# Seven block products in layer 2 for two of four experts, layer 1 in longer periods, activation sums on GpSimd

## The chip, the cores and the metric

The kernel runs on one core of one Trainium2 chip. The metric is the device time of one execution in microseconds (us); a kernel's figure is the median of its runs. Before the change it was 541.23 us (three runs, 541.15 to 541.62). All numbers below come from those timings, or from one profiled execution per kernel. Chips differ a little, so the kernel before ran beside every experiment on the same chip.

The engines are called TensorE (PE in the profile, its weight loads PEld), VectorE (DVE), ScalarE (ACT), GpSimd (POOL) and SyncE (SP, which here only issues DMA).

## The reference

Linear attention for 8 batches of 8 heads, followed by a mixture of four experts over 4608 tokens of 512 features.

```python
def phi(x):                               # feature map
    return np.where(x > 0, x, np.exp(x) - 1.0) + 1.0
# q, k, v: (8, 8, 576, 64)
kv  = einsum('bhsd,bhse->bhde', phi(k), v);  z = sum(phi(k), axis=2)
num = einsum('bhsd,bhde->bhse', phi(q), kv); den = einsum('bhsd,bhd->bhs', phi(q), z) + 1e-6
x   = (num / den) transposed to (4608, 512)
p   = domain_probs / (domain_probs.sum(-1) + 1e-9)
out = sum over e of p[:, e] * (max(x @ w1[e], 0) @ w2[e])   # w1: 4 x 512 x 1024, w2: 4 x 1024 x 512
```

The kernel cuts the tokens into nine tiles of 512. Tiles 0 to 7 are the first 512 rows of each batch. Tile 8 is made of the 64 rows that each batch has left ("leftover" rows). A *unit* is one tile and one expert, written (tile, expert); the experts are 0 to 3. Attention of batch j+1 is done in small steps between the products of tile j. Tile 0 and unit (1,0) are plain start-up work.

## The kernel before: the parts that matter

Layer 1 of a unit is done, from unit (1,1) on, with seven block products instead of eight (Winograd's form of Strassen's scheme): x and w1 are cut into 2 x 2 blocks, some sums of blocks are made beforehand (`token_sums` for x on GpSimd, `weight_sums` for w1 once), and the results are combined when they leave the accumulator (PSUM). A block row of 128 hidden features is called a chunk here. Layer 2 is plain: four token quarters, eight products each.

```python
def token_sums(j):                       # 4 instructions on GpSimd per tile
    ...
    nc.gpsimd.tensor_tensor(out=t[:, 0], in0=b12, in1=b11, op=AO.subtract)
    ...
class Block:                             # one chunk: 7 products of 2 x (128x256)
    def a(self):
        product(self.b, a_block(e, 0, 0, k), x[:, 0:2, 0:NH], True)
        u1 = self.copy("u1")             # ScalarE, 128x256
        product(self.e5, ...); product(pa2, ...)
        add_relu(self.h1[:, 0:NH], pa2, u1)   # VectorE, 128x256
    # b6, c, d: the other four products
def layer2_half(j, e, ns, hT, half):     # plain layer 2, 4 of 8 products of 128x512
    for fj in range(half * FC // 2, (half + 1) * FC // 2):
        nc.tensor.matmul(out=py, lhsT=hT[fj][:, ns * P : (ns + 1) * P], rhs=w2_sb[e][:, fj, :], ...)
    ...
    nc.vector.scalar_tensor_tensor(out=acc, in0=py, scalar=pscal, in1=acc, op0=AO.mult, op1=AO.add)
# feature map: exp on ScalarE, max(x,0)+1 on GpSimd, the minimum of both on VectorE
eng.tensor_scalar(dst, src, 0.0, 1.0, AO.max, AO.add)          # eng = GpSimd
nc.vector.tensor_tensor(out=dst, in0=ee[:, 0:n], in1=dst, op=AO.min)
```

Of the kernel before, what the change touches and what calls it, by code (L numbers as in the profile page):

```python
# [20 lines left out]
def kernel(  # L21
# [16 lines left out]
    P = 128  # L38
# [13 lines left out]
    NHT = 18  # L52
    NACC = 5
    NH = NT // 2
    FH = FC // 2
    BIG = 3.0e38
# [6 lines left out]
    warm_in = pconst.tile([P, NT], FP16, tag="warm", name="warm_in")  # L63
    nc.vector.memset(warm_in, 0.0)


    NB2 = 2
    kvzs, kls, qls = [], [], []
    for i in range(NB2):
        kl = pconst.tile([P, NPAIR, P], FP16, tag=f"kl{i}", name=f"kl{i}")  # L70
        nc.vector.memset(kl, 0.0)
        kls.append(kl)
        kvz = pconst.tile([P, NPAIR, 2, DE], FP16, tag=f"kvz{i}", name=f"kvz{i}")
        nc.vector.memset(kvz, 0.0)
        kvzs.append(kvz)
        qTl = pconst.tile([P, 2, 2, P], FP16, tag=f"ql{i}", name=f"ql{i}")
        nc.gpsimd.memset(qTl, 0.0)
        qls.append(qTl)
# [10 lines left out]

    px = ctx.enter_context(tc.tile_pool(name="px", bufs=1))  # L90
    xT_left = px.tile([P, DC, NT], FP16, tag="xTl")

    praw = ctx.enter_context(tc.tile_pool(name="praw", bufs=6))
# [61 lines left out]
    class Batch:  # L155
# [19 lines left out]
        def load(self, name, g, eng=nc.sync, parts=1):  # L175
            src = {"q": q, "k": k, "v": v}[name]
            t = praw.tile([P, HG, CM, D], FP32, tag="raw", name="rawb")
# [9 lines left out]
        def alloc(self):  # L187
# [3 lines left out]
            self.vl = pa.tile([P, HG, DE], FP16, tag="vl", bufs=2, name="vl")  # L191
# [4 lines left out]
            self.x = pa.tile([P, NPAIR, CM, P], FP16, tag="xsb", bufs=1, name="x_sb")  # L196
# [3 lines left out]
        def phi(self, name, g, part=0, parts=1, eng=nc.vector):  # L200

            n = HG // parts
            h0 = g * HG + part * n
            src = self.raw[name, g][:, part * n : (part + 1) * n]
            dst = (self.qp if name == "q" else self.kp)[:, :, h0 : h0 + n, :]
            dst = dst.rearrange("p c h d -> p h c d")
            ee = pa.tile([P, HG, CM, D], FP16, tag="phie", bufs=2, name="ee")
            nc.scalar.activation(ee[:, 0:n], src, AF.Exp)  # L208
            eng.tensor_scalar(dst, src, 0.0, 1.0, AO.max, AO.add)  # L209
            nc.vector.tensor_tensor(out=dst, in0=ee[:, 0:n], in1=dst, op=AO.min)  # L210
# [9 lines left out]
        def left_kv(self):  # L220
            el = pa.tile([P, HG * D], FP16, tag="el", bufs=2, name="el")
            kt = pa.tile([P, HG * D], FP16, tag="ktl", bufs=1, name="ktl")
            rk = self.rl[:, 0].rearrange("p h d -> p (h d)")
            nc.scalar.activation(el, rk, AF.Exp)
            nc.gpsimd.tensor_scalar(kt, rk, 0.0, 1.0, AO.max, AO.add)
            for u in range(2):
                us = slice(u * HP, (u + 1) * HP)
                nc.vector.tensor_tensor(
                    out=self.kl[us, 2 * u : 2 * u + 2].rearrange("p a d -> p (a d)"),
                    in0=el[us],  # L230
                    in1=kt[us],
                    op=AO.min,
                )
            nc.gpsimd.tensor_copy(self.vl[:, :, 0:D], self.rl[:, 1])

        def left_q(self, eng=nc.vector):
            el = pa.tile([P, HG * D], FP16, tag="el", bufs=2, name="elq")
# [3 lines left out]
            eng.tensor_scalar(qd, rq, 0.0, 1.0, AO.max, AO.add)  # L241
# [61 lines left out]
        def nd(self, i0, n):  # L303

            ps = aps([P, 3, 2, DE], FP32, "psum_nd")
# [56 lines left out]
    def layer1_group(j, e, fj, hT, ph=None, dcs=range(DC)):  # L362
# [10 lines left out]
        if dcs[-1] == DC - 1:  # L373
            ht = pm.tile([P, NT], FP16, tag="ht", bufs=NHT, name="ht")
            nc.scalar.activation(ht, ph, AF.Relu)  # L375
            hT.append(ht)
        return ph

    pys = {}

    def layer2_half(j, e, ns, hT, half):
        if half == 0:
            pys[ns] = ppm.tile([P, Dm], FP32, tag="py", bufs=2, name="py")
        py = pys[ns]
        for fj in range(half * FC // 2, (half + 1) * FC // 2):
            nc.tensor.matmul(  # L386
                out=py,
                lhsT=hT[fj][:, ns * P : (ns + 1) * P],
# [4 lines left out]
        if half == 0:  # L393
            return
        if e == 0:
            accs[j, ns] = pm.tile([P, Dm], FP32, tag="acc", bufs=NACC, name="acc")
        acc = accs[j, ns]
        pscal = p_sb[:, j, ns, e : e + 1]
        if e == 0:
            nc.scalar.activation(acc, py, AF.Identity, scale=pscal)  # L400
        else:
            nc.vector.scalar_tensor_tensor(  # L402
                out=acc,
                in0=py,
                scalar=pscal,
                in1=acc,
                op0=AO.mult,
                op1=AO.add,
            )
        if e == E - 1:  # L410
            if j < B:
                nc.sync.dma_start(
                    out=out_b[j, 0:SM].rearrange("(p c) d -> c p d", c=CM)[ns],
                    in_=acc,
                )
            else:
                for u in range(2):
                    nc.sync.dma_start(
                        out=out_b[2 * ns + u, SM:S],
                        in_=acc[u * HP : (u + 1) * HP],  # L420
                    )
# [10 lines left out]
    def weight_sums(e, part):  # L432
# [8 lines left out]
        else:  # L441
            nc.vector.tensor_tensor(
                out=w[:, 0:2, f2], in0=w[:, 0:2, f1], in1=w[:, 0:2, f2], op=AO.subtract
            )

# [27 lines left out]
    class Block:  # L473


        def __init__(self, j, e, k, hT):
            self.j, self.e, self.k, self.hT = j, e, k, hT

        def copy(self, tag):
            u = pm.tile([P, NH], FP32, tag=tag, bufs=2, name=tag)  # L480
# [3 lines left out]
        def a(self):  # L484
            j, e, k = self.j, self.e, self.k
            x, t = xT_of(j), tts[j]
            self.b = ppm.tile([P, NT], FP32, tag="b", bufs=2, name="pb")[:, 0:NH]
            self.e5 = ppm.tile([P, NT], FP32, tag="e", bufs=2, name="pe")[:, 0:NH]
            pa2 = ppm.tile([P, NT], FP32, tag="s", bufs=2, name="pa2")[:, 0:NH]
            self.h1 = pm.tile([P, NT], FP16, tag="ht", bufs=NHT, name="ht1")  # L490
            self.h2 = pm.tile([P, NT], FP16, tag="ht", bufs=NHT, name="ht2")
            self.hT[k], self.hT[FH + k] = self.h1, self.h2
            product(self.b, a_block(e, 0, 0, k), x[:, 0:2, 0:NH], True)
            u1 = self.copy("u1")
            product(self.e5, s_block(e, 0, k), t[:, 0], True)
            product(pa2, a_block(e, 0, 1, k), x[:, 2:4, 0:NH], True)
            add_relu(self.h1[:, 0:NH], pa2, u1)

        def b6(self):
            product(self.b, s_block(self.e, 1, self.k), tts[self.j][:, 1], False)  # L500
            self.u2 = self.copy("u2")

        def c(self):
            product(self.b, a_block(self.e, 1, 0, self.k), tts[self.j][:, 2], False)
            u3 = self.copy("u3")
            add_relu(self.h2[:, NH:NT], self.e5, u3)

        def d(self):
            e, k = self.e, self.k
            product(self.b, a_block(e, 1, 1, k), tts[self.j][:, 3], False)  # L510
            nc.scalar.activation(self.h2[:, 0:NH], self.b, AF.Relu)
            product(self.e5, s_block(e, 2, k), xT_of(self.j)[:, 2:4, NH:NT], False)
            add_relu(self.h1[:, NH:NT], self.e5, self.u2)
# [5 lines left out]
    def layer2(j, e, hT):  # L519
        return [(layer2_half, j, e, ns, hT, h) for ns in range(NSUB) for h in range(2)]  # L520

    def unit(j, e, hT=None, phs=()):

        hT = [] if hT is None else hT
        return layer1(j, e, hT, phs) + layer2(j, e, hT)

    def run(pieces, steps=(), lead=0):

        n, m = len(pieces) - lead, len(steps)
        done = 0  # L530
        for i, g in enumerate(pieces):
            g[0](*g[1:])
            while done < m and (i + 1 - lead) * m >= (done + 1) * n:
                steps[done][0](*steps[done][1:])
                done += 1

    ORDER = [("q", 0), ("k", 0), ("v", 0), ("q", 1), ("k", 1), ("v", 1)]

    def batch_steps(bt, nxt):


        def load(n, g):
            if nxt is not None:
# [6 lines left out]
        def nd(i0, n):  # L550
# [6 lines left out]
            [(bt.phi, n, g, part, 2, nc.gpsimd)] + ([(load, n, g)] if part else [])  # L557
# [6 lines left out]
        for i in range(4):  # L564
            st[2 + i].append((bt.vcast, i // 2, i % 2, 2))
            if i % 2:
                st[2 + i].append((load, "v", i // 2))
        st.append([(bt.left_kv,)])
        st.append([(bt.left_q, nc.gpsimd), (load_left,), (bt.dma_qTl,), (bt.kv, 0)])
        for i0 in range(0, NPAIR * CM, 3):  # L570
            st.append([(nd, i0, min(3, NPAIR * CM - i0))])
        st[10].append((bt.kv, 2))
# [3 lines left out]
    def warm(n):  # L576

        warm_ps = ppm.tile([P, NT], FP32, tag="py", bufs=2, name="warm_ps")
        for i in range(n):
            nc.tensor.matmul(  # L580
                out=warm_ps, lhsT=warm_in[:, 0:P], rhs=warm_in, start=True, stop=True
# [4 lines left out]
    with tc.manual_schedule(  # L586
# [19 lines left out]
        b0.phi("q", 1, eng=nc.gpsimd)  # L606
# [24 lines left out]
        hT = []  # L631
# [34 lines left out]
        for i, g in enumerate(pieces):  # L666
# [3 lines left out]
            if r in (1, 3, 5) and e == 3:  # L670
                weight_sums(e, r // 2)
            elif r in (9, 11, 13) and e < 3:
                weight_sums(e, r // 2 - 4)
            elif r == 15 and e in (1, 2):
                weight_sums(e, 3)
            while done < len(steps) and T0 + TG * (i + 1) >= steps[done][0]:
# [5 lines left out]
        hT = []  # L682
# [10 lines left out]
        for n, g in ORDER:  # L693
# [4 lines left out]
        for g in layer1(1, 0, hT, phs):  # L698
            g[0](*g[1:])
        weight_sums(0, 3)  # L700
        weight_sums(3, 3)
        turn["aps"], turn["ph"] = ["s"], None


        l2 = layer2(1, 0, hT)
        units = [(j, e) for j in range(1, NTILES) for e in range(E) if (j, e) > (1, 0)]
        blocks = []
# [84 lines left out]
```

## Time and profile before

| before | value | read from |
|---|---|---|
| median | 541.23 us | timings |
| span profiled | 539.9 us, granted clock 0.98 | page |
| TensorE busy | 95% | page, part 1 |
| one unit without attention work (tiles 7, 8) | 13.02 us | timeline: spacing of the first products of units |
| one tile with attention work (2, 4, 5, 6; tile 3 took 56.29) | 55.88 us | the same |

First the busy times on the page (part 1: us busy, share of the span, instructions), and the chain of waits by engine (part 4).

```profile
PE 512.7 (95%) x3449; PEld 324.3 (60%) x3449; DVE 316.0 (59%) x718; ACT 286.1 (53%) x722; POOL 173.8 (32%) x158
...
PE 76%; DMA 11%; ACT 3%; DVE 3%; issue 3%; POOL 2%; SPq 1%; DVEq 0%; ACTq 0%; POOLq 0%
```

TensorE is the bound: it is busy nearly all the time, and 76% of the chain that ended last is its work. A matmul's end is modelled in the profile, so rates are read from starts. Here is TensorE's timeline in tile 7 (start us, us, engine, line, operation; x2 means two products merged).

```profile
440.23 0.38 PE L386 MATMUL py<-w_0_84,ht_5630 128*128 128x512 f16 x1
440.45 0.38 PE L386 MATMUL py<-w_0_84,ht_5669 128*128 128x512 f16 x1
...
441.10 0.38 PE L461 MATMUL pb<-xT,w_1_81 128*128 128x256 f16 x2
441.31 0.38 PE L461 MATMUL pe<-tt,s_1_90 128*128 128x256 f16 x2
```

A product of 512 columns takes 0.217 us and one of 256 columns 0.108 us (two in 0.217), with no gaps. Layer 2 of a unit is therefore 32 x 0.217 = 6.93 us. Three groups of the two engines that the change loads (last figures: us busy, mean ns of one, then idle time before them):

```profile
L402 DVE SCALAR_TENSOR_TENSOR acc<-py,p_sb,acc 128x512 f32<-128x512 f32 x108 | 81.0, 750 | 54.5 <-PE py L386 54.3
L453 POOL TENSOR_TENSOR tt<-xT 128x512 f16<-128x512 f16 x7 | 8.1, 1156 | 172.2 <-DMA xT<-x_sb 156.3
...
L209 POOL TENSOR_SCALAR kp<-rawb 128x512 f16<-128x512 f32 x24 | 45.5, 1922 | 0.0
```

VectorE adds a quarter of layer 2 in 0.750 us; GpSimd makes one token sum in 1.156 us, and a share of a feature map in 1.922 us.

### The profile page before, as it was taken

To read this page: it belongs to the slowest core of one execution; us is meant where nothing else is said; L and a number is where in the kernel's file an instruction comes from. 1 tells how busy PE (TensorE), PEld (TensorE's weight loads), DVE (VectorE), ACT (ScalarE), POOL (GpSimd) and SP (SyncE) were. 2 spreads that over 40 slices of the span, in tenths; PEclk is the share of its full clock that TensorE was granted. 3 is DMA by queue.
4 is the path that set the end of the run, shared out by engine and by line. 5 is a ranking of instruction groups with operands and counts; after the bars stand their busy time and mean duration, and the time that the engine had idled before them with its cause. 6 is when DMAs were issued, how large, how long until landed. Compare 5 with 4: busy or idle time off the path is not lost.

```text
span 539.9 us, 9645 instructions
## 1 busy us (share of the span) xinstructions
PE 512.7 (95%) x3449; PEld 324.3 (60%) x3449; DVE 316.0 (59%) x718; ACT 286.1 (53%) x722; POOL 173.8 (32%) x158
## 2 busy tenths in 40 slices
PE   6599998989999999999999999999999999999996
PEld 2344454556666666666666666666666666666662
DVE  4422486457664767476756675667656655655463
ACT  5354375683576357544764476446754455445540
POOL 4722512930960195008600780059003300000000
PEclk9599999999999999999999999999999999999999
DMA  9999935675165206710472039200511010011003
GB/s 262 135 208 209 237 125 182 168 224 126 38 185 168 41 6 162 221 33 16 126 244 46 16 93 264 59 17 31 87 26 26 20 59 2 1 38 42 2 0 79
DMA packets 80736, 54.31 MB, mean 101 GB/s; under 512 B 46032, under 2 KB 73680, under 8 KB 80688
## 3 DMA queue, kind: packets, MB, share of 16 engines
q1 hardware_dynamic: 71648, 41.77, 29.1%
q0 software_dynamic: 9040, 11.93, 11.7%
q8 instruction: 27, 0.44, 0.4%
q14 instruction: 21, 0.17, 0.1%
HBM read 45.16 MB, written 9.44 MB: 101 GB/s over the span
## 4 chain that ended last, share of the span: by engine, by line
PE 76%; DMA 11%; ACT 3%; DVE 3%; issue 3%; POOL 2%; SPq 1%; DVEq 0%; ACTq 0%; POOLq 0%
PE py L386 39%; PE pb L461 18%; PE pe L461 10%; DMA w_3_87<-in_moe_w_dram 4%; DMA w_1_85<-in_moe_w_dram 3%; DMA rawb<-in_q_dram 2%; ACT ee L208 1%; PE psum_nd L308 1%; PE ph L366 1%; DMA ql_75<-qlp 1%; DMA rl<-in_k_dram 1%; SPq L168 1%; PE psum_kv L273 1%; POOL qp L209 1%; DVE x_sb L296 1%
## 5 line engine op out<-in xcount | busy, mean ns | idle before, releaser
L402 DVE SCALAR_TENSOR_TENSOR acc<-py,p_sb,acc 128x512 f32<-128x512 f32 x108 | 81.0, 750 | 54.5 <-PE py L386 54.3
L453 POOL TENSOR_TENSOR tt<-xT 128x512 f16<-128x512 f16 x7 | 8.1, 1156 | 172.2 <-DMA xT<-x_sb 156.3
L209 POOL TENSOR_SCALAR qp<-rawb 128x512 f16<-128x512 f32 (+1 forms) x25 | 49.4, 1998 | 1.0 <-DMA rawb<-in_q_dram 1.0
L209 POOL TENSOR_SCALAR kp<-rawb 128x512 f16<-128x512 f32 x24 | 45.5, 1922 | 0.0
L208 ACT ACTIVATE ee<-rawb 128x512 f16<-128x512 f32 (+1 forms) x56 | 37.9, 692 | 3.6 <-DMA rawb<-in_q_dram 2.6
L400 ACT ACTIVATE acc<-py,p_sb 128x512 f32<-128x512 f32 x36 | 24.7, 687 | 23.7 <-PE py L386 23.7
L375 ACT ACTIVATE ht<-ph 128x512 f16<-128x512 f32 x40 | 23.2, 598 | 21.7 <-PE ph L366 21.5
L461 PEld LDWEIGHTS <-w_1_81 128*128 128x128 f16 x256 | 25.0, 98 | 9.8
L461 PEld LDWEIGHTS <-w_3_83 128*128 128x128 f16 x256 | 24.6, 98 | 8.0
L461 PEld LDWEIGHTS <-w_2_82 128*128 128x128 f16 x256 | 24.4, 98 | 8.2 <-issue 2.5
L461 PEld LDWEIGHTS <-w_0_80 128*128 128x128 f16 x224 | 21.9, 98 | 8.5
L296 DVE TENSOR_TENSOR x_sb<-psum_nd,recip 128x384 f16<-128x384 f32 (+2 forms) x52 | 25.2, 485 | 1.8
L461 PEld LDWEIGHTS <-s_1_90 128*128 128x128 f16 x192 | 18.7, 98 | 11.0 <-issue 2.3
L386 PEld LDWEIGHTS <-ht 128*128 128x128 f16 x160 | 15.3, 98 | 15.6
L461 PE MATMUL pb<-tt,w_2_82 128*128 128x256 f16 x128 | 24.4, 273 | 0.0
L461 PE MATMUL pb<-tt,w_3_83 128*128 128x256 f16 x128 | 24.4, 273 | 0.0
L461 PE MATMUL pb<-tt,w_1_81 128*128 128x256 f16 x128 | 24.4, 272 | 0.0
L461 PEld LDWEIGHTS <-s_3_92 128*128 128x128 f16 x192 | 18.7, 98 | 8.5
L461 PEld LDWEIGHTS <-s_0_89 128*128 128x128 f16 x168 | 16.4, 98 | 9.5 <-issue 1.3
L210 DVE TENSOR_TENSOR qp<-ee,qp 128x512 f16<-128x512 f16 (+1 forms) x28 | 14.8, 545 | 12.2 <-ACT ee L208 5.4
L461 PEld LDWEIGHTS <-s_2_91 128*128 128x128 f16 x192 | 18.1, 98 | 6.1 <-issue 0.5
L461 PE MATMUL pb<-tt,w_0_80 128*128 128x256 f16 x112 | 21.4, 273 | 0.0
(1621 smaller groups left out, 1406.1 us busy)
## 6 DMA issues: line engine op xcount, KB each, us to landing
out_dram<-acc SPq DMA_DIRECT2D x32, 256.0 KB, 2.5
rawb<-in_q_dram SPq DMA_DIRECT2D x14, 512.0 KB, 4.2
rawb<-in_k_dram SPq DMA_DIRECT2D x14, 512.0 KB, 6.3
rawb<-in_v_dram SPq DMA_DIRECT2D x13, 512.0 KB, 5.7
w_0_80<-in_moe_w_dram POOLq DMA_DIRECT2D x4, 256.0 KB, 7.0
w_0_84<-in_moe_w_dram POOLq DMA_DIRECT2D x2, 512.0 KB, 11.0
w_1_81<-in_moe_w_dram POOLq DMA_DIRECT2D x2, 512.0 KB, 15.0
w_1_85<-in_moe_w_dram POOLq DMA_DIRECT2D x2, 512.0 KB, 18.8
```

Of the source, the lines that this page charges most:

```text
L168: eng.dma_start(out=self.rl[u * HP : (u + 1) * HP, i], in_=src[b, u * HG : (u + 1) * HG, SM:S].rearrange("h r d -> r h d"),)
L208: nc.scalar.activation(ee[:, 0:n], src, AF.Exp)
L209: eng.tensor_scalar(dst, src, 0.0, 1.0, AO.max, AO.add)
L210: nc.vector.tensor_tensor(out=dst, in0=ee[:, 0:n], in1=dst, op=AO.min)
L273: nc.tensor.matmul(out=ps[:, i], lhsT=self.kp[:, c, hs], rhs=self.vp[:, c, hs], start=(c == 0), stop=False,)
L296: nc.vector.tensor_tensor(out=dst.rearrange("p n (u d) -> p n u d", u=2), in0=ps[:, 0:n, :, 0:D], in1=recip[:, 0:n].broadcast_to([P, n, 2, ...
L375: nc.scalar.activation(ht, ph, AF.Relu)
L386: nc.tensor.matmul(out=py, lhsT=hT[fj][:, ns * P : (ns + 1) * P], rhs=w2_sb[e][:, fj, :], start=(fj == 0), stop=(fj == FC - 1),)
L400: nc.scalar.activation(acc, py, AF.Identity, scale=pscal)
L402: nc.vector.scalar_tensor_tensor(out=acc, in0=py, scalar=pscal, in1=acc, op0=AO.mult, op1=AO.add,)
L453: nc.gpsimd.tensor_tensor(out=t[:, 0], in0=b12, in1=b11, op=AO.subtract)
L461: nc.tensor.matmul(out=ps, lhsT=lhsT(kc), rhs=rhs[:, kc], start=first and kc == 0, stop=kc == 1, skip_group_check=True,)
```

## The change

The intent is to take TensorE time out of layer 2, as layer 1 already does. For experts 1 and 3 (`SE`) layer 2 is also done by seven block products: 56 products of 256 columns instead of 32 of 512. To do so GpSimd makes four sums of activations per half unit (`hidden_sums`), and VectorE adds each of 14 half-bank results into the output. Layer 1 goes from one to two chunks per PSUM bank (fewer, larger copies and sums). The feature maps leave GpSimd for VectorE and ScalarE. Layer 2 follows layer 1 half a unit behind instead of a quarter.

```diff
+    SE = (1, 3)
...
+    def hidden_sums(h):
+        hs = pm.tile([P, 3, 2, NH], FP16, tag="hs", bufs=2, name="hs")
+        a11, a21 = h[:, :, 0, 0:NH], h[:, :, 0, NH:NT]
+        a12, a22 = h[:, :, 1, 0:NH], h[:, :, 1, NH:NT]
+        nc.gpsimd.tensor_tensor(out=hs[:, 0], in0=a21, in1=a22, op=AO.add)
+        nc.gpsimd.tensor_tensor(out=hs[:, 1], in0=hs[:, 0], in1=a11, op=AO.subtract)
+        nc.gpsimd.tensor_tensor(out=a21, in0=a11, in1=a21, op=AO.subtract)
+        nc.gpsimd.tensor_tensor(out=hs[:, 2], in0=a12, in1=hs[:, 1], op=AO.subtract)
+    def layer2_product(j, e, hT, hss, p, i):      # product p of token half-quarter i
+        if p == 2:
+            pys[i] = new_py()                     # one bank for all seven products of i
+        run, side = pys[i][:, 0:DH], pys[i][:, DH:Dm]
+        ...                                       # 4 products of 128x256, then one add
+        add_acc(j, e, ns, ps, ds, False)          # VectorE, 128x256
...
         def phi(self, name, g, part=0, parts=1):
...
-            eng.tensor_scalar(dst, src, 0.0, 1.0, AO.max, AO.add)
-            nc.vector.tensor_tensor(out=dst, in0=ee[:, 0:n], in1=dst, op=AO.min)
+            if self.b < 3:
+                nc.vector.tensor_scalar(dsth, src, 1.0, 1.0, AO.add, AO.max)
+                nc.vector.tensor_tensor(out=dsth, in0=eeh, in1=dsth, op=AO.min)
+            else:
+                nc.scalar.activation(dsth, src, AF.Identity, bias=1.0)
+                nc.vector.scalar_tensor_tensor(
+                    out=dst, in0=dst, scalar=1.0, in1=ee, op0=AO.max, op1=AO.min)
...
+        NSLOT, LAG = 7, 6                         # a unit is 14 slots
+                for d in range(2):
+                    work[at + (d - 1) * NSLOT].append((sums, d))
+                l2 = [(layer2_product, j, e, hT, hss, p, i) for p in (2, 5, 1, 6, 7, 3, 4) for i in range(2)]
...
-        b0.phi("q", 1, eng=nc.gpsimd)
+        b0.phi("q", 1)
```

Also changed: input buffers 6 to 4, output accumulators (`acc`) 5 to 4, one buffer instead of two for leftover k, q and v and for k'v, x in buffers shared with other tiles, leftover k and q to VectorE, k'v of a batch in one step.

## The prediction

> **What bounds it now.** TensorE: on the page busy 95% of the 539.9 us span at a granted clock of 0.98, and 76% of the chain of waits. In the timeline of tiles 7 and 8 (no attention work) a 128x256 product takes 0.108 us, a 128x512 one 0.217 us, without gaps: 13.03 us per (tile, expert) unit. A batch period with attention work is 55.9 us (spacing of equal pieces in the chain); 4 x 13.0 plus about 2.2 us of attention products leave 1.6 us lost per batch. The waits show part of it (ScalarE copy of k'v 0.6 us, VectorE 0.3 us).
>
> **What it removes.** Layer 2 of one unit is 32 products of 512 columns, 6.93 us. Seven block products are 56 of 256 columns, 6.07 us. That saves 0.87 us in 16 units: 13.9 us, all on TensorE and so on the critical path. Weight loads (98 ns) still hide behind 108 ns products, as layer 1 shows.
>
> **What it adds and moves.**
> - VectorE: 14 scaled adds of 128x256 instead of 4 of 128x512 (0.750 us each; estimate for half the elements 0.48 us): 6.8 instead of 3.0 us per such unit. Layer 1's sums, 6 of 512 instead of 12 of 256, save about 0.9 us per unit. Feature-map work comes over from GpSimd. VectorE goes from 36 to about 42 us per batch of 53, and to about 95% in units with seven products and attention work. The Trainium skill, "VectorE: DVE Perf Modes", perf-mode tier table, puts fp32 PSUM operands at 1x; 0.750 us for 512 columns agrees.
> - ScalarE: about even, 32 us per batch.
> - GpSimd: loses 16 maxima of 1.92 us per batch, gains 8 hidden sums per such unit; token sums of that size take 1.155 us, so 9.2 us per unit of 12.6. The Trainium skill, "GPSIMD Engine Reference", section 3.1, gives about 2.6 cycles per element for two inputs; the trace agrees.
>
> **New waits.** The products of a token half accumulate in one bank, so VectorE must have read a half bank before TensorE returns two slots (1.7 us) later; after product and add about 0.55 us of queueing is allowed. At 95% some of it is missed: 0.65 us on 12 units, 8 us in all. The first hidden sum has about 2.6 us, its chain needs about 2.3. At the very end nothing covers it: +0.6 us.
>
> **Regained.** Layer 1 in longer periods gives copies more slack, and k'v comes a step ahead of its use: about 5 us. At the start GpSimd's 3.63 us pass, which delayed the weight loads and x, goes to VectorE (0.69 us): about 2 us, less if DMA, saturated there, gives nothing back, or if four input buffers instead of six delay batch 1.
>
> **Sum.** 541.2 - 13.9 - 5 - 2 + 8 = about 528 us; range 519 to 538. Chances: faster by over 2% 0.60, within 2% 0.36, slower 0.04.
>
> **What would show it.** Right: in tiles 7 and 8 two units cost 12.15 and two 13.0 us; batch period 52.5 to 54; TensorE's waits in the batches name VectorE's adds into acc; GpSimd 23 us per batch; first layer 1 product 2 us sooner. Wrong: product spacing over 0.108 us in layer 2; batch period near 55.
>
> **What would make it wrong.** VectorE over 100% in units 1 and 3, or slowed by GpSimd's reads (in this trace a VectorE sum beside GpSimd work took 1.10 instead of 0.68 us): then 540. Hidden sums late behind the token sums: a stall per tile. Or fewer waits than I think: then 519.

## The result, and the profile after

The changed kernel takes 541.48 us (median of four runs, 539.74 to 542.04); the kernel before took 541.42 us beside it. The ratio is 0.9996, with a 95% interval of 0.9972 to 1.002: the same. Here and below a ratio is the mean time of one kernel's fast runs over that of the other's of the same rounds, so it is not quite the ratio of the medians quoted.

The page of the changed kernel, the same two lines as before:

```profile
PE 503.6 (93%) x3833; PEld 363.0 (67%) x3833; DVE 366.7 (68%) x729; ACT 279.8 (52%) x514; POOL 215.0 (40%) x221
...
PE 76%; DVE 11%; issue 4%; DMA 3%; ACT 3%; POOL 1%; SPq 0%; DVEq 0%; ACTq 0%; POOLq 0%
```

The span is 539.5 us. TensorE has less to do, and VectorE's share of the chain has gone from 3% to 11%. The equal 76% of TensorE misleads: until 97 us, before unit (1,1), the chain of the kernel before runs 51 us through DMA (weight loads mostly) and that of the changed kernel 12 us, with TensorE's products in their place. From 97 us on TensorE's part fell from 402 to 351 us and VectorE's rose from 8 to 49 us (the chain of `--critical`, summed). That says where to look; what was lost is read below from the lengths of units. The groups that answer to those above:

```profile
L423 DVE SCALAR_TENSOR_TENSOR acc<-py,p_sb,acc 128x256 f32<-128x256 f32 (+1 forms) x268 | 137.7, 522 | 28.5 <-PE py L512 18.4
L486 POOL TENSOR_TENSOR hs<-h 128x512 f16<-128x512 f16 x32 | 37.0, 1158 | 198.2 <-DVE h L560 198.2
```

The costs of the instructions were as foreseen: 1.158 us per hidden sum, and 0.475 us per 128x256 add (the mean of the group within tile 3). So the question is where the time went. The table gives the start of layer 1 of a unit, taken from TensorE's timeline (its first product `pb<-xT`), as differences between the kernels.

| stretch | before | after | difference |
|---|---|---|---|
| start to (1,1) | 96.91 | 94.91 | -2.00 |
| (1,1) to (2,0) | 44.87 | 49.77 | +4.90 |
| (2,0) to (7,0), five tiles | 279.78 | 273.78 | -6.00 |
| (7,0) to (8,3), seven units | 91.15 | 88.36 | -2.79 |
| (8,3) to the end of the span | 27.16 | 32.64 | +5.48 |

(About 1.1 us of the last row is no loss. It is an estimate from the product times: layer 2 follows a quarter unit later than before, so more of it is left when the last layer 1 begins, and so are three products of a block of layer 1 that is now twice as large. Each column is one trace; the first row is within the scatter of such traces, see the experiments.) In tiles 7 and 8 a unit takes 12.62 instead of 13.02 us, that is 0.80 us less for each pair of units: the saving of the products is there. It is lost in three other places.

**Place 1: unit (1,2) takes 22.81 instead of 18.02 us.** TensorE's and then GpSimd's timeline there:

```profile
116.78 0.39 PE L282 MATMUL psum_kv<-vp,kp 128*128 128x130 f16 x4
123.19 0.27 PE L289 MATMUL psum_kv<-vl,kl_63 128*128 128x130 f16 x1 [6.02 <-POOL vl L243]
```

```profile
118.03 1.15 POOL L486 TENSOR_TENSOR hs<-h 128x512 f16<-128x512 f16 x1 [1.49 <-DVE h L560]
119.26 1.15 POOL L487 TENSOR_TENSOR hs<-hs,h 128x512 f16<-128x512 f16 x1
120.37 1.20 POOL L488 TENSOR_TENSOR h<-h 128x512 f16<-128x512 f16 x1
121.53 1.20 POOL L489 TENSOR_TENSOR hs<-h,hs 128x512 f16<-128x512 f16 x1
122.68 0.46 POOL L243 CAST vl<-rl 128x256 f16<-128x256 f32 x1
```

TensorE stands still for 6.02 us before the product of batch 2's leftover rows. It needs `vl`, a cast of 0.46 us on GpSimd that stands in GpSimd's queue behind the hidden sums of unit (1,1), which themselves wait for late results of layer 1. The Trainium skill, "PSUM — Partial Sum Buffer", section "Engine vs sequencer instructions", calls the queues of ScalarE, VectorE and GpSimd strictly first in, first out, and this trace agrees: the cast's input had been loaded long before (issued at 91.35 us), and it started 0.05 us before the last sum ended and not sooner.

The pause is not all that unit (1,2) lost. TensorE's granted clock fell while it stood still (`--windows`):

```profile
core 0: us, PE busy (x) PEld busy (x) DVE busy (x) ACT busy (x) POOL busy (x), PEclk, DMA share, GB/s
120.80:127.40 6.60, 4.21 (x30) 3.58 (x30) 3.91 (x8) 1.95 (x6) 2.34 (x3) 0.50 0.35 90
```

At this clock of 0.50 four products of 256 columns were 0.85 us apart (124.88 and 125.73) instead of 0.435. From the spacing of its starts the unit's 22.81 us are about 10.7 of products at full clock, 9.7 of waits (6.2 at this pause, 3.5 at layer 1's sums and copies before it) and 2.3 of slower products: an estimate.

**Place 2: unit (j,0) of each tile 2 to 6 takes 14.23 us.** Its products need about 12.6 us (an estimate from 0.435 us per four of 256 columns and 0.217 us per one of 512). Waits of TensorE from 85 to 535 us (total us, times, longest), the changed kernel:

```profile
PE py L512 <- DVE acc L423: 6.1, 12, 0.8
PE psum_kv L289 <- POOL vl L243: 6.0, 1, 6.0
```

TensorE returns to a bank before VectorE has read it. From start to start unit (3,0) lost 1.64 us against its products' times, and unit (3,1), which takes 13.01 us, another 0.42. VectorE's timeline at the longest such wait, in unit (3,0), and below it GpSimd's:

```profile
210.88 0.47 DVE L423 SCALAR_TENSOR_TENSOR acc<-py,p_sb,acc 128x256 f32<-128x256 f32 x1
211.28 1.50 DVE L222 SCALAR_TENSOR_TENSOR qp<-qp,ee 128x512 f16<-128x512 f16 x1
212.70 0.86 DVE L423 SCALAR_TENSOR_TENSOR acc<-py,p_sb,acc 128x256 f32<-128x256 f32 x2
```

```profile
208.31 1.68 POOL L487 TENSOR_TENSOR hs<-hs,h 128x512 f16<-128x512 f16 x1
209.96 1.16 POOL L488 TENSOR_TENSOR h<-h 128x512 f16<-128x512 f16 x1
211.07 1.16 POOL L489 TENSOR_TENSOR hs<-h,hs 128x512 f16<-128x512 f16 x1
212.17 0.87 POOL L243 CAST vl<-rl 128x256 f16<-128x256 f32 x1
```

The feature map's instruction on VectorE (L222, two operands in SBUF) usually takes 0.69 us. Here it took 1.50: it began 0.21 us after a hidden sum had begun, and the sum ended at 212.23, so 0.95 of the 1.50 us fell beside it. Then GpSimd's cast, begun at 212.17, took 0.87 instead of 0.46 us. This fits the Trainium skill, "SBUF — State Buffer", section "Who interferes with whom": a VectorE instruction with two SBUF inputs and a GpSimd instruction that reads SBUF exclude each other for the whole of the one that came first. The adds from PSUM, with only one tensor input in SBUF, are not touched (0.475 us on average in tile 3, and the same 0.475 us in run 8 below, where GpSimd's sums are short), as that section also says.

**Place 3: the end.** The chain of waits over the last products of unit (8,3):

```profile
525.38 0.61 PE py L512 x4
...
526.01 0.49 DVE acc L423
...
526.55 0.61 PE py L512 x4
...
527.18 0.49 DVE acc L423
...
527.72 0.61 PE py L512 x4
```

TensorE and VectorE take turns. Each of the two banks is filled in 0.61 us (four products and their way out), then read in 0.49 us, then filled again: 1.17 us per turn, in which TensorE has only 2 x 0.43 = 0.87 us of work. With no layer 1 beside it nothing fills the gap; over seven turns about 2.1 us are lost. At the end all four results become ready together, and SyncE's queue issues eight stores one behind the other (first fence: before, second fence: after; from the timeline of SP, where the second figure is the length of the whole group).

```profile
530.81 6.29 SPq L418 DMA_DIRECT2D out_dram<-acc  x8
```

```profile
531.65 5.04 SPq L410 DMA_DIRECT2D out_dram<-acc  x8
```

Before, VectorE's last add ended at 535.97 and the span 3.9 us later; after, it ended at 533.53 and the span 5.9 us later, with the stores still being issued.

### The profile page after: what moved, and what is told of

Same layout as the page of the kernel before. It is cut to its first block, busy times and chain, and to the rows that moved or that the text cites. A ratio compares the mean times of both kernels' runs of the same rounds, so it can differ in the third digit from the quotient of the medians.

```text
span 539.5 us, 10086 instructions
## 1 busy us (share of the span) xinstructions
PE 503.6 (93%) x3833; PEld 363.0 (67%) x3833; DVE 366.7 (68%) x729; ACT 279.8 (52%) x514; POOL 215.0 (40%) x221
## 4 chain that ended last, share of the span: by engine, by line
PE 76%; DVE 11%; issue 4%; DMA 3%; ACT 3%; POOL 1%; SPq 0%; DVEq 0%; ACTq 0%; POOLq 0%
PE py L432 24%; PE pb L576 16%; PE py L512 14%; PE pe L576 8%; PE ph L377 6%; PE ps L576 4%; DVE acc L423 4%; DVE h L560 2%; DVE qp L222 1%; PE psum_kv L282 1%; DMA xT<-x_sb 1%; DVE x_sb L305 1%; ACT ee L215 1%; DMA rawb<-in_v_dram 1%; PE psum_nd L319 1%
## 5 line engine op out<-in xcount | busy, mean ns | idle before, releaser
L423 DVE SCALAR_TENSOR_TENSOR acc<-py,p_sb,acc 128x256 f32<-128x256 f32 (+1 forms) x268 | 137.7, 522 | 28.5 <-PE py L512 18.4
L486 POOL TENSOR_TENSOR hs<-h 128x512 f16<-128x512 f16 x32 | 37.0, 1158 | 198.2 <-DVE h L560 198.2
L432 PEld LDWEIGHTS <-h 128*128 128x128 f16 x640 | 62.3, 98 | 29.7
L432 PE MATMUL py<-w_2_78,h 128*128 128x512 f16 x288 | 79.9, 379 | 0.0
L432 PE MATMUL py<-w_0_76,h 128*128 128x512 f16 x288 | 78.9, 379 | 0.0
L512 PEld LDWEIGHTS <-h 128*128 128x128 f16 x512 | 49.9, 97 | 12.8 <-issue 5.8
L512 PEld LDWEIGHTS <-hs 128*128 128x128 f16 x384 | 37.7, 98 | 10.3 <-issue 5.7
L487 POOL TENSOR_TENSOR hs<-hs,h 128x512 f16<-128x512 f16 x32 | 39.7, 1239 | 2.5
L489 POOL TENSOR_TENSOR hs<-h,hs 128x512 f16<-128x512 f16 x32 | 37.2, 1161 | 0.0
L488 POOL TENSOR_TENSOR h<-h 128x512 f16<-128x512 f16 x32 | 37.1, 1161 | 0.0
L576 PEld LDWEIGHTS <-w_1_73 128*128 128x128 f16 x256 | 24.7, 98 | 11.7 <-ACT u_1111 L587 1.3
L576 PEld LDWEIGHTS <-w_3_75 128*128 128x128 f16 x256 | 24.5, 98 | 11.2
L512 PE MATMUL py<-w_3_79,h 128*128 128x256 f16 x192 | 28.7, 272 | 2.3 <-DVE acc L423 2.0
L576 PEld LDWEIGHTS <-w_2_74 128*128 128x128 f16 x256 | 24.5, 99 | 7.3 <-issue 1.1
L512 PE MATMUL py<-w_1_77,h 128*128 128x256 f16 x192 | 28.8, 273 | 0.0
L576 PEld LDWEIGHTS <-w_0_72 128*128 128x128 f16 x224 | 21.9, 98 | 7.0
```

What stands on the lines that cost most here:

```text
L423: nc.vector.scalar_tensor_tensor(out=acc, in0=ps, scalar=pscal, in1=acc, op0=AO.mult, op1=AO.add)
L432: nc.tensor.matmul(out=py, lhsT=rows(hT, fj)[:, ns * P : (ns + 1) * P], rhs=w2_sb[e][:, fj, :], start=(fj == 0), stop=(fj == FC - 1),)
L486: nc.gpsimd.tensor_tensor(out=hs[:, 0], in0=a21, in1=a22, op=AO.add)
L487: nc.gpsimd.tensor_tensor(out=hs[:, 1], in0=hs[:, 0], in1=a11, op=AO.subtract)
L488: nc.gpsimd.tensor_tensor(out=a21, in0=a11, in1=a21, op=AO.subtract)
L489: nc.gpsimd.tensor_tensor(out=hs[:, 2], in0=a12, in1=hs[:, 1], op=AO.subtract)
```

## The experiments

Twelve kernels ran. Two theories were at issue. The first: the products save what they should, and the gain is lost in the three places, each through an order or a buffer that can be changed. The rival: seven products cost what they cost (VectorE's total load, or weight loads), wherever they stand. Starts of (1,1) varied between 94.25 and 97.72 us over the traces of these kernels, so single places are compared by lengths of units, not by totals.

### 1. vl_scalar: batch 2's cast of leftover v on ScalarE

```diff
-            nc.gpsimd.tensor_copy(self.vl[:, :, 0:D], self.rl[:, 1])
+            (nc.scalar.copy if self.b == 2 else nc.gpsimd.tensor_copy)(self.vl[:, :, 0:D], self.rl[:, 1])
```

> The copy of batch 2's leftover rows of v (vl) goes from GpSimd to ScalarE, nothing else. Theory: the 6.0 us wait of TensorE at about 117 to 123 us is GpSimd's order (the copy stands behind eight hidden sums that wait for TensorE's own later work), so the wait goes, unit (1,2) falls from 22.8 us to about 17, the total to about 536 us. Rival: VectorE, slowed beside GpSimd in the same stretch (leftover k at 118 to 122 us), is just as late, so k'v waits for kl in place of vl and at most 1 or 2 us are gained (540).

Measured: 539.08 us, ratio 0.9974; unit (1,2) 21.04 us. The rival of this run was the better guess. Waits of TensorE in this kernel:

```profile
PE psum_kv L292 <- DVE kl L242: 3.6, 2, 2.2
```

The same product now waits for leftover k on VectorE. Its four instructions there took 0.28, 1.07, 1.21 and 1.12 us (timeline) beside the hidden sums, where they take 0.28 us undisturbed. Two engines were late behind one cause, and the profile had named only the one that came last. The clock fell here too (0.50 from 119.4 to 126.0 us), so that part of the loss stayed.

### 2. se12: experts 1 and 2 instead of 1 and 3

```diff
-    SE = (1, 3)
+    SE = (1, 2)
```

> Experts 1 and 2 instead of 1 and 3 get seven products; same number of products, sums and adds. Theory: what the batches lose is lost where expert 3's layer 2 meets the feature maps of the next batch on VectorE (first unit of a tile 14.2 us where 12.6 of products are), so the batch period falls from 54.76 to about 53 us, 8 us in all for tiles 2 to 6; and the last unit, now with eight products, ends without half-bank waits and with stores spread out, about 4 us less: total near 529. Rival: seven products cost what they cost (VectorE's total load, or weight loads of 98 ns beside 108 ns products), wherever they stand: period 54.5 or more, only the end is won: 537.

Measured: 542.97 us, ratio 1.0045. A miss in the total, yet unit (j,0) fell from 14.23 to 13.07 us, as the theory said. Unit (j,3) rose from 12.91 to 13.96 us by a new wait:

```profile
PE py L512 <- POOL hs L486: 10.2, 8, 1.5
```

With neighbouring experts the first hidden sum of the second unit waited until the first unit's last product had read its buffer: `hs` is one tile with two buffers, both in use until the last product that reads it (p = 3) ends. In the GpSimd timeline that sum started at 193.37, after 5.65 us of idling:

```profile
193.37 1.15 POOL L486 TENSOR_TENSOR hs<-h 128x512 f16<-128x512 f16 x1 [5.65 <-DVE h L560]
```

The profile names a VectorE sum as the releaser, which ended at 193.34; the last product that reads `hs` began at 192.91 and ended about then too. That it was the buffer is shown by runs 4 and 6. So this run does not decide between theory and rival by its total; run 6 does.

### 3. se12_vl: both

> Both of the changes before. Theory: they add up, 6 and 12 us: about 523 us. Rival: the stall of batch 2 is already changed by the other choice of experts or comes back elsewhere: over 527.

Measured: 540.93 us, ratio 1.0009. The expected sum failed for the reasons of runs 1 and 2; units (1,2) and (j,3) took 21.62 and 13.96 us.

### 4. last_plain: another order of experts in tile 8 alone

```diff
+        units += [(NTILES - 1, e) for e in (0, 1, 3, 2)]     # tile 8 stores after expert 2
```

> As the changed kernel, but in tile 8 the experts run in order 0, 1, 3, 2, so the last unit of all has eight products per token quarter. Theory: the end of the changed kernel loses about 4.4 us (TensorE and VectorE taking turns on half banks 2 to 2.6 us, eight stores issued one after the other in the last 5 us about 1.8 us), so the total falls to about 537.5 us, with batch period 54.76 as before. Rival: the end is long only because layer 2 follows later (more is left when the last layer 1 ends): then no gain.

Measured: 539.41 us, ratio 0.998, interval 0.9961 to 0.9999. The stretch from (8,3) to the end fell from 32.64 to 30.4 us, with the batch period unchanged (54.75). That is less than the 4.4 us expected, since the same buffer wait of 1.5 us appeared once here too (experts 1 and 3 were neighbours in tile 8). The two together make 3.7 us. Here the profile names the product that still read the buffer:

```profile
POOL hs L489 <- PE py L515: 5.4, 1, 5.4
PE py L515 <- POOL hs L489: 1.5, 1, 1.5
```

### 5. left_early: batch 2's leftover k and v in its first step

```diff
-        st.append([(bt.left_kv,)])
+        if bt.b == 2: st[0].insert(1, (bt.left_kv,))
+        else: st.append([(bt.left_kv,)])
```

> Experts 1 and 3 as in the changed kernel; only batch 2's leftover k and v are prepared in the first step of that batch, before any hidden sum is issued. Theory: the stall of TensorE at 117 to 123 us has two halves that overlap, the copy of v queued behind hidden sums on GpSimd (6.0 us) and the leftover k on VectorE, whose four short instructions take 1.1 us each beside GpSimd (3.6 us remained with the copy on ScalarE). Done early both are gone: unit (1,2) falls from 22.8 us to about 16.5, the total by 5 to 6 us. Rival: the stall is that of the whole squeezed batch (18 steps in 42 slots) and moves to the feature maps of k: at most the 2 us of before.

Measured: 536.64 us, ratio 0.9932. Unit (1,2) fell from 22.81 to 16.60 us, unit (1,1) rose from 13.35 to 13.98. So the stall was one of order, and both its halves went; with them went the fall of the clock (1.00 from 110 to 135 us). A rest stayed: layer 1 then waited up to 2.7 us for VectorE, whose feature maps of batch 2 stood beside the hidden sums (that these were the reason is argued, not shown).

### 6. se12_hs3: the hidden sums in three tiles

```diff
-    SE = (1, 3)
+    SE = (1, 2)
-        hs = pm.tile([P, 3, 2, NH], FP16, tag="hs", bufs=2, name="hs")
+        hs = [pm.tile([P, 2, NH], FP16, tag=f"hs{i}", bufs=2, name=f"hs{i}") for i in range(3)]
```

> Experts 1 and 2, and the hidden sums in three small tiles of two buffers each instead of one tile of two buffers (same bytes). Theory: with neighbouring experts the first sum of the second had to wait until the first expert's last product had read its buffer, 1.5 us of TensorE per tile, 8 times; with three tiles each comes free as its own product is done. So the wait for GpSimd's hs goes and unit (j,3) falls from 13.96 to about 12.4 us, the period to about 53.2, the total from 543 to about 531. Rival: GpSimd itself is too slow for 16 sums in two units and the wait stays over 1 us.

Measured: 530.70 us, ratio 0.9823, interval 0.9799 to 0.9847. Unit (j,3) took 12.51 us and the wait for GpSimd's sums was gone. The period is 13.07 + 13.02 + 14.61 + 12.52 = 53.2 us instead of 54.76, with the same number of products, adds and sums. The rival theory (the load itself) falls here. The stretch from (8,3) to the end was 28.8 us. Waits of TensorE from 85 us on:

```profile
PE psum_kv L289 <- POOL vl L243: 6.1, 1, 6.1
PE pe L576 <- DVE h L560: 1.8, 2, 1.5
PE pb L576 <- ACT u L587: 1.4, 2, 1.0
PE py L432 <- DVE acc L423: 1.4, 5, 0.3
```

Place 1 is untouched by it, places 2 and 3 are mostly gone.

### 7. se12_hs3_left: runs 5 and 6 together

> The two together: about 525 us, which beats both kernels. Rival: what was a wait on one becomes a wait on another, over 530.

Measured: 526.79 us, ratio 0.9749, interval 0.9725 to 0.9772. The two repairs add up.

### 8. sums_small: short hidden sums

```diff
-        hs = pm.tile([P, 3, 2, NH], FP16, tag="hs", bufs=2, name="hs")
-        a11, a21 = h[:, :, 0, 0:NH], h[:, :, 0, NH:NT]
+        full, m = hs_two[d], 32            # two zeroed tiles; 32 of 256 columns are summed
+        hs = full[:, :, :, 0:m]
+        a11, a21 = h[:, :, 0, 0:m], h[:, :, 0, NH:NH + m]
```

> Wrong result on purpose: the changed kernel with experts 1 and 3, but the hidden sums on GpSimd take 32 of 256 columns (the rest is zeros), so the instructions are there and short. It separates two theories of the 1.6 us that unit (j,0) loses where expert 3's layer 2 meets the feature maps. Theory: the maps' sums on VectorE, which read two operands in SBUF, are held up by GpSimd's reads (1.2 and 1.5 us instead of 0.69); then they fall to 0.69 and (j,0) falls from 14.23 to 13.2 us or less, the stall of batch 2 falls too. Rival: VectorE is simply overbooked in these slots; then (j,0) stays over 14 us. (The tiles cost two more memsets at the start, so the total is not compared, only units.)

Measured (one look): wrong result, as meant; unit (j,0) 13.59 us, unit (1,2) 16.21 us. The feature map's instruction by tile, first in the changed kernel, then in this one (min/median/max of its duration in ns):

```profile
L222 DVE SCALAR_TENSOR_TENSOR qp<-qp,ee x20: 691/946/1506, 149.2 to 375.5; 128x512 f16<-128x512 f16 x20
```

```profile
L222 DVE SCALAR_TENSOR_TENSOR qp<-qp,ee x20: 675/686/885, 143.4 to 367.4; 128x512 f16<-128x512 f16 x20
```

Both theories of this run have a part. GpSimd's long sums account for 14.23 - 13.59 = 0.64 us of each (j,0). Unit (1,2) lost 6.6 us of its length, but there the short sums also clear GpSimd's queue before the cast, so this run doesn't tell reads from order. About 1.0 us in (j,0) was left to explain.

### 9. no_maps: the feature maps of batches 3 to 7 without their last VectorE instruction

```diff
-                nc.vector.scalar_tensor_tensor(
-                    out=dst, in0=dst, scalar=1.0, in1=ee, op0=AO.max, op1=AO.min)
+                pass
```

> Wrong result on purpose: the changed kernel without the last VectorE instruction of the feature maps of batches 3 to 7 (8 per batch); hidden sums are whole. With short hidden sums unit (j,0) fell from 14.23 to 13.59 us, so 0.64 us of its loss is GpSimd's reads holding up these instructions; the theory is that the rest is the same instructions taking VectorE's time in the slots of expert 3's seven products. Then (j,0) falls to 12.6 or 12.7 us in tiles 2 to 6, what its products need, and the batch period to about 53.1. Rival: the adds of the seven products and layer 1's sums overbook VectorE alone; then (j,0) stays over 13.2 us.

Measured (one look): unit (j,0) 12.76 us and unit (j,1) 12.62 instead of 13.01; the period is 52.9 us. Waits for VectorE's adds from 130 to 420 us, the changed kernel and this one:

```profile
PE py L512 <- DVE acc L423: 5.6, 11, 0.8
PE py L510 <- DVE acc L421: 0.2, 1, 0.2
```

(The result passed the comparison, though the function is no longer the reference's: x+1 is near exp(x) for inputs this small.) So with the maps' last instruction away, the adds of the seven products and layer 1's sums alone do not overbook VectorE. Of about 2.0 us that a tile lost against its products' times, 1.85 came back. Since run 2 brought (j,0) down to 13.07 us with the maps in place and expert 3 plain, the loss is the meeting of these eight instructions with expert 3's products. By subtraction of two runs with one look each, 0.64 us of it comes through GpSimd and the rest through the instructions' own time.

### 10. before_q1dve: the kernel before, one line of the change

```diff
-        b0.phi("q", 1, eng=nc.gpsimd)
+        b0.phi("q", 1)
```

> The kernel before with one line of the change: the second half of batch 0's q goes to VectorE instead of GpSimd. Theory: GpSimd's 3.63 us pass there held up both the weight loads and x; with it gone the first layer 1 product comes at about 21 us instead of 24.2 and the gain is kept up to the end: about 538.5 us. Rival: the loads are bound by DMA and tile 0 to tile 1 waits for batch 1's inputs, so the 3 us are given back: 541.

Measured: 538.41 us, ratio 0.9966, interval 0.9951 to 0.9981. The first product of layer 1 came at 21.07 instead of 24.17 us, and in the timings about 1.8 us (0.34% of 541) were kept. This one line alone gives about the 2 us that were predicted for the start. The first product of layer 1, before and here:

```profile
24.17 1.87 PE L366 MATMUL ph<-xT,w_0_80 128*128 128x512 f16 x4 [2.58 <-DMA xT<-x_sb]
21.07 1.87 PE L366 MATMUL ph<-xT,w 128*128 128x512 f16 x4 [2.29 <-DMA xT<-x_sb]
```

### 11. stores_two: the last stores from two queues

```diff
-                nc.sync.dma_start(
+                (nc.scalar if u else nc.sync).dma_start(
```

> The changed kernel; of the last eight stores every second is issued by ScalarE instead of SyncE. Theory: the four results of tile 8 become ready within 2.4 us, and eight issues of about 0.63 us in one queue take 5.0 us; in two queues they take half, so the end comes about 1.8 us sooner (539.5 where the changed kernel has 541.3). Rival: the transfers themselves take the time, no gain.

Measured: 540.71 us, ratio 1.0006, interval 0.9974 to 1.0039: no difference that the timings could show. In the trace four stores in each queue took 2.52 and 2.81 us to issue instead of 5.04 for eight, but each landed later (2.7 and 3.3 us after its issue instead of 2.3), and the span ended 5.1 instead of 5.9 us after VectorE's last add. This agrees with the Trainium skill, "Trainium Kernel Development and Optimization", section "Key Constraints": queues of several engines share the same DMA engines and save only issue time. That the issue takes part in the end is thus likely, but it was not shown in a time. What is shown of place 3 is that a plain last unit brings most of it back (runs 4 and 6), which changes the turns on the banks and the readiness of the four results together.

### 12. combined: a version that beats both kernels

Run 6, the stores of run 11, and unit (1,1) with eight products, so that no hidden sums stand beside batch 2.

```diff
-            if e in SE:
+            if e in SE and n > 0:                  # n == 0 is unit (1,1)
...
+            if n == 0:                             # expert 1's last weight difference, made in place
+                work[at + 2 * NSLOT + 2].append((weight_sums2, e, 3))
```

> Experts 1 and 2 with seven products and hidden sums in three tiles (530.7 us), stores from two queues, and unit (1,1) with eight products (expert 1's last weight difference is then taken after it), since there the hidden sums of unit (1,1) slow the squeezed batch 2 on VectorE. Theory: unit (1,2) falls from 22.7 to about 14.5 us at the price of 0.87 us, the total to about 523 us, below the 526.8 us of the version with the leftovers done early. Rival: batch 2 in 42 slots stalls without hidden sums too (18.0 us in the kernel before): 526 or more.

Measured: 524.65 us (523.85 to 526.94), ratio 0.9722, interval 0.9693 to 0.9752, correct. Unit (1,2) took 15.62 us, more than the 14.5 expected. Its page and its longest waits from 85 us on:

```profile
PE 498.3 (95%) x3809; PEld 358.3 (69%) x3809; DVE 355.4 (68%) x719; ACT 280.3 (54%) x514; POOL 200.7 (38%) x213
...
PE 86%; DVE 7%; DMA 3%; ACT 2%; issue 1%; SPq 1%; DVEq 0%; ACTq 0%
```

```profile
PE pe L576 <- DVE h L560: 1.5, 1, 1.5
PE pb L576 <- ACT u L587: 1.4, 2, 1.0
```

TensorE's share of the chain has risen from 76% to 86%. VectorE has nearly the load of the changed kernel (355 against 367 us busy), and the kernel is 2.8% faster than the one before: what counted most was where that load stands (run 6 shows it with the same number of instructions). Against run 7, on another chip, the intervals overlap.

## Why the prediction was wrong

It said 528 us with a range of 519 to 538; 541.48 was measured. The sign that it had set against itself, a batch period near 55 us, is what came (54.76). The step that failed is the term of new waits, 8 us and 0.6 at the end: at its 0.65 us per unit that was 6.5 us in tiles 2 to 6, 1.3 us in tile 1 and 0.6 us at the end, where about 9, 8 and 4.4 us were measured. Point by point, with the measured size beside it:

- *"That saves 0.87 us in 16 units: 13.9 us, all on TensorE."* Right, a little high: two units of tiles 7 and 8 take 25.24 instead of 26.04 us, 0.80 us less per unit with seven products, 12.8 us in all. (The prediction looked for two units of 12.15 and two of 13.0; since layer 2 follows half a unit behind, each shows the mean of the two, 12.62.)
- *"Regained ... about 5 us", and k'v a step ahead.* The size was about right. In run 6, with all work in place, the period is 53.2 us, where 55.88 less two savings of 0.80 would be 54.3: 1.1 us of old waits per tile are gone, 5 us in five tiles. Without the maps' instruction (run 9, one look, less work) it is 52.9 us, which makes 1.4 us per tile and 7 in all. Whether the longer periods or the earlier k'v did it was not tested.
- *"At the start ... about 2 us."* Right by run 10: the one line alone gave 1.8 us in the timings. The 2.00 us of the table would not show it, since (1,1) began anywhere from 94.5 to 97.7 us in the traces of kernels with this start.
- *The costs of single instructions* (0.48 us per add, 1.155 us per sum, 42 us of VectorE per batch): right; VectorE was busy 42.1 us from 200 to 255 us, GpSimd 24.4.
- *"New waits ... 0.65 us on 12 units, 8 us in all."* The mechanism was named (VectorE late at a bank, slowed by GpSimd's reads) and the size was near: 1.85 us per tile, 9 us in tiles 2 to 6. But the wait does not lie evenly on all units with seven products. It lies where expert 3's products meet the feature maps, while expert 1's unit, beside the attention's normalisation, lost nothing to speak of: (j,2) and (j,3) take 14.61 and 12.91 us, an estimate from their product times being 14.6 and 12.9. I had counted VectorE's load and not its place. The prediction's own warning, "slowed by GpSimd's reads ...: then 540", comes close to 541 by luck: of about 21 us of new losses GpSimd's long sums explain some 0.64 us per tile in tiles 2 to 6, and in batch 2 a part that no run separates.
- *"At the very end nothing covers it: +0.6 us."* Wrong size. Against the products' time the end lost about 4.4 us (5.48 less the estimated 1.1 of deferred work), and 3.8 of them came back with a plain last unit (run 6). I had counted the first hidden sum only, and neither the turns on two banks, which cost 2.1 us by the chain, nor that four results become ready together.
- *The step that failed most: that nothing new would stall in batch 2.* The prediction feared hidden sums late behind token sums, and named the four input buffers as a danger to batch 1. It did not look for small old work behind the hidden sums in GpSimd's queue. The stall of 6.0 us in unit (1,2), the waits around it and about 2.3 us of products at half the clock made the stretch (1,1) to (2,0) about 8 us longer than the products' times would have it (an estimate: +4.90 measured, where about -3.2 was due, through cheaper and later layer 2 and the larger block of layer 1 left over). Undone by order alone in run 5, and by a plain unit (1,1) in run 12.

As a sum: -12.8 for the products, -7 regained and -2 at the start make -22. Against it stand about 9 us in tiles 2 to 6, 8 us in tile 1 and 4.4 us at the end. That leaves nothing. (The 7 and the 9 both start from run 9's period; what the two kernels measure is their difference, about 2 us.)

What stays open: how the end's loss divides between the turns on the banks and the issue of stores (run 11 could not be told from no change), the waits for layer 1's sums and copies that are left in unit (1,2) of the last version (15.62 us), and why the clock fell in the pause of unit (1,2).

## What to carry to other kernels

When work moves to an engine whose queue also carries small old tasks that TensorE needs soon, go through that queue in program order and ask what each small task will now stand behind. A busy share like VectorE's here (42.1 of 55 us, 77%) does not tell whether an accumulator comes free in time: find the stretch where two bursts on that engine meet, and move one of them (here another choice of expert, at the same cost, was worth 1.5 us per tile once its buffers allowed it). After such a move look for the buffer whose lifetime the old place had hidden, and split a tile by its parts' lifetimes before giving it more memory.

## What the Trainium skill lacked or had wrong

- "SBUF — State Buffer", "Who interferes with whom", words its rule for any VectorE instruction with two SBUF inputs, but names only `tensor_tensor`, `tensor_scalar`, the copies and `tensor_reduce`; the three-operand form on VectorE (scalar and two fp16 tensors in SBUF) is not named there. In these runs it behaves the same way: 0.69 us alone, up to 1.51 us beside a GpSimd sum of 1.16 us, and 0.69 again (median) when the sums were cut to an eighth.
- "VectorE: DVE Perf Modes", "The perf-mode tier table", has no row for that form either (the skill's microarchitecture page remarks on its throughput, without a time). On fp16 in SBUF it took 0.69 us for 512 columns, where the two-operand minimum took 0.42 us; from PSUM 0.475 us for 256 and 0.746 us for 512 columns.
- "Trainium Kernel Development and Optimization", "Key Constraints", says that several queues save only issue time. That section gives no size: eight stores of 128 KB took 5.04 us to issue from one queue and 2.52 and 2.81 us from two, and landed 0.4 to 1.0 us later each.
